# The order of the first loads: w1's first row split over two queues behind the x tiles, bias rows later

## The chip, the cores and the metric

The kernel runs on one core of one Trainium2 chip. The metric is the device time of one execution in microseconds; lower is better. A core has TensorE (PE in the profile, its weight loads apart as PEld), VectorE (DVE), ScalarE (ACT), GpSimd (POOL), and SyncE (SP), which here only issues DMAs. ScalarE can issue DMAs too, on a queue of its own, in order with its other instructions. All DMAs run on the same 16 DMA engines.

## The reference

```python
x = A_x                                           # 1 x 2048 x 512, bf16
g = sigmoid((x * gate_w).sum(-1, keepdims=True))
# a: linear attention, 32 heads of 16; phi(t) = where(t > 0, t + 1, exp(t)) + 1e-6
q, k, v = split(x @ wqkv)
o = (phi(q) @ (phi(k)^T v)) / (phi(q) . sum(phi(k)) + 1e-6)
a = o @ wo
# b: MLP over the tokens, F = 1792
h = layernorm(x)                                  # over the 512 features
u = gelu(einsum("bsd,sf->bdf", h, w1) + b1)
b = (einsum("bdf,fs->bds", u, w2) + b2) transposed back
return g * a + (1 - g) * b
```

## The kernel before

The 2048 tokens are 16 tiles of 128 (`NT`), the 512 features 4 blocks (`ND`), and the 1792 columns of w1 14 blocks of 128 (`NF`). The program has these stages, and TensorE goes through them in this order:

- 18 warm-up matmuls on a constant tile (L185), which need no data.
- MLP 1, first part (L277 to L283): u's first 8 blocks (`NFA`), accumulated in 8 PSUM banks over the 16 token tiles. Step t of the loop takes one token tile: 8 matmuls, one for each block of 128 columns of w1's row block t, all with the normalised tile `xh[:, t, :]`. The first 12 tiles go tile by tile; for the last 4 the order is block by block, so that each bank can be finished and its GELU started.
- k and the Gram product (L320 to L329), from x turned by DMA transposes and from `pk`.
- the other 6 blocks of MLP 1, mixed with q (L476 to L498), then y = u times w2 with the attention's product added into the same banks (L548 to L564).

Here "w1's row t" is the 128 x 1024 part that step t takes (`w1A[:, t, :]`, 256 KB in bf16), and its "blocks" 0 to 7 are the 128 columns each that the 8 matmuls take as weights. Every matmul goes through one helper, so all of TensorE's work is line L74; every DMA goes through `load`, line L124.

LayerNorm runs on VectorE and ScalarE, one tile after the other: `ln_bn` (BATCH_NORM_STATS, L195) reads the x tile, `ln_aggr` (L198) makes mean and variance, ScalarE takes the square root (L200), then `ln_apply` makes the reciprocal (L206) and `xh` (L208). The work on VectorE is in an order written by hand (`pin` keeps the program's order): the first half of tile t + 1's statistics stands in front of tile t's reciprocal and apply for t = 0 and t = 2.

The loads at the start, all of the functions named above being called in this order:

- ScalarE's queue: b1's rows (3.5 KB) into `b_rows`, then block 0 of w1's row 0 (32 KB), then an activation on one column (L136) whose only use is that the square root's table is loaded early.
- SyncE's queue: x tile 0, x tile 1 (128 KB each), blocks 1 to 7 of w1's row 0 (224 KB), w1's row 1, x tile 2, x tile 3, w1's row 2, and from there x tile t + 1 and w1's row t in turn. b2's rows stand behind w1's row 4. Behind them come the gate's weights, wk, 16 transposes of x, w1's other columns, wv, wo and wq.

The loads of the first loop wait for no data. The DMAs share eight semaphores, which are given out in turn, so that each waits until the one eight before it has landed.

`b_rows` holds b1 and b2 as rows; at tile 8 of LayerNorm, VectorE turns them into columns (L234 to L236), which GELU and the last scaling use.

w2's second half (columns 1024 to 2047) comes in pieces of its 14 row blocks while VectorE normalises q tile by tile (L508 to L514). It takes the place of w1's other columns, so its first piece waits for their last reader. Between the pieces stand the stores of q (`q_dram`) and, every four tiles, the transposes that bring q back (`turn`). The first y tile that reads the second half is tile 8.

Of the kernel before, what the change touches and what calls it, by code (L numbers as in the profile page):

```python
# [15 lines left out]
def kernel(  # L16
# [13 lines left out]
    nc = tc.nc  # L30
    P = nc.NUM_PARTITIONS
# [11 lines left out]
    NF = F // P  # L43
# [4 lines left out]
    FA = NFA * P  # L48
# [5 lines left out]
    w1_view = B_w1.rearrange("(t p) f -> p t f", p=P)  # L54
    w2_view = B_w2.rearrange("(f p) s -> p f s", p=P)
    b1_view = B_b1.rearrange("(f p) -> f p", p=P)
# [9 lines left out]
    def ptile(shape, dt, name):  # L66
        return persist.tile(shape, dt, name=name, tag=name)
# [27 lines left out]
    b_rows = ptile([32, P], BF16, "b_rows")  # L95
# [22 lines left out]
    w1A = wpool.tile([P, NT, FA], BF16, name="w1A", tag="w1st")  # L118
# [4 lines left out]
    def load(o, i, eng=None, **kw):  # L123
        pin((eng or nc.sync).dma_start(out=o, in_=i, **kw))  # L124

    def load_x(t0, t1):
        load(xr[:, t0:t1, :], x_view[:, t0:t1, :])

    def load_w1a(t):
        load(w1A[:, t, :], w1_view[:, t, 0:FA])  # L130


    tbl = work.tile([P, 1], FP32, name="tbl", tag="tbl", bufs=2)
    load(b_rows[0:NF, :], b1_view, nc.scalar)
    load(w1A[:, 0, 0:P], w1_view[:, 0, 0:P], nc.scalar)
    pin(nc.scalar.activation(out=tbl[:], in_=eps_t[:], func=ACT.Sqrt))  # L136

    load_x(0, 1)
    load_x(1, 2)
    load(w1A[:, 0, P:FA], w1_view[:, 0, P:FA])  # L140
    load_w1a(1)
    load_x(2, 3)
    for t in range(2, NT):
        if t + 1 < NT:
            load_x(t + 1, t + 2)
        load_w1a(t)
        if t == 4:
            load(b_rows[NF : NF + NT, :], b2_view)
    load(gw_b[:], gw_row_view.to_broadcast([P, D]))
    load(wk_sb[:], wqkv_view[:, :, D : 2 * D])  # L150
# [354 lines left out]

    pieces = {0: ((0, 4), (4, 7)), 5: ((7, 9),), 7: ((9, NF),)}  # L508
    for t in range(12):
        normalise(t)  # L510
        if t % 4 == 3:
# [83 lines left out]
```

## Time and profile before

| | |
|---|---|
| time before, median of 3 runs | 163.27 us (162.86 to 163.67) |
| the profiled execution | 163.07 us |
| its span, first to last instruction | 161.4 us |
| clock granted to TensorE | full |
| TensorE busy | 157.6 us (98%) |
| VectorE, ScalarE busy | 118.7 us (74%), 53.1 us (33%) |
| first matmul of MLP 1 | at 4.99 us |
| last matmul | ends at 158.5 us |
| DMA moved | 28.33 MB, mean 176 GB/s |

The profile is one execution; its times are microseconds from the first instruction. A group's line gives the engine, the operation, what is written and read, how often, and the idle time before it with what ended it. `SPq` and `ACTq` are the issues of DMAs on the two queues: the time in such a row is the issue alone, and the tile's own view gives the time from issue to landing. The share of busy time on TensorE is that of a pipelined engine whose ends are modelled: a matmul of 512 columns shows as 0.38 us, but the next one starts 0.216 us after it.

### The profile page before, as it was taken

How to read it: one execution, taken by the hardware profiler on the slowest of the kernel's cores; microseconds unless marked ns; L12 is line 12 of the kernel's file. 1: busy time of each engine (PE TensorE's matmuls, PEld its weight loads, DVE VectorE, ACT ScalarE, POOL GpSimd, SP SyncE). 2: the span in 40 equal slices, each digit the busy share in tenths (PEclk: the TensorE clock that was granted, in tenths of full speed). 3: DMA queues.
4: the chain of work that ended last, by engine and by line, in shares of the span. 5: the costliest groups of instructions: out<-in, count | busy, mean ns of one | idle time of the engine just before them, and what ended most of it. 6: DMA issues, size and time to landing. Idle time of an engine off the chain costs nothing.

```text
span 161.4 us, 2274 instructions
## 1 busy us (share of the span) xinstructions
PE 157.6 (98%) x820; PEld 73.1 (45%) x820; DVE 118.7 (74%) x278; ACT 53.1 (33%) x89; POOL 1.2 (1%) x8
## 2 busy tenths in 40 slices
PE   7999999999999999999999999999999999999993
PEld 5444444444444444444444444444444444444452
DVE  2799998959999998899895999999999970000002
ACT  4122227794342321434225970000008300550050
POOL 2000000000000000000000000000000000000000
PEclk9999999999999999999999999999999999999999
DMA  4999999444699630229952007826525935744421
GB/s 124 308 342 351 341 283 149 108 103 106 158 391 391 149 123 0 87 50 300 399 214 67 0 33 262 290 66 154 174 65 124 340 89 126 230 143 100 151 98 33
DMA packets 36838, 28.33 MB, mean 176 GB/s; under 512 B 20444, under 2 KB 31196, under 8 KB 36828
## 3 DMA queue, kind: packets, MB, share of 16 engines
q1 hardware_dynamic: 36384, 27.90, 57.6%
q10 hardware_dynamic: 444, 0.30, 0.6%
q8 instruction: 6, 0.10, 0.3%
q14 instruction: 4, 0.03, 0.0%
HBM read 19.28 MB, written 4.46 MB: 147 GB/s over the span
## 4 chain that ended last, share of the span: by engine, by line
PE 95%; DMA 2%; ACTq 0%; DVE 0%; issue 0%; DVEq 0%
PE yps L74 39%; PE accA L74 17%; PE accB L74 13%; PE qacc L74 9%; PE Gps L74 9%; PE kacc L74 9%; DMA w1A<-in_B_w_dram 2%; ACTq L124 0%; PE kvps L74 0%; DVE ot L539 0%; PE w2ps L74 0%; DVE b_rows L114 0%; DVEq L539 0%; DVE eps_t L115 0%
## 5 line engine op out<-in xcount | busy, mean ns | idle before, releaser
L74 PE MATMUL yps<-uT,w2h 128*128 128x512 bf16 (+2 forms) x238 | 49.2, 366 | 0.0
L74 PEld LDWEIGHTS <-w2h 128*128 128x128 bf16 x238 | 22.8, 98 | 25.9
L74 PE MATMUL accA<-xh,w1A 128*128 128x512 bf16 x128 | 28.0, 381 | 0.1
L532 ACT ACTIVATE ot<-yps,c,c 128x512 bf16<-128x512 f32 x15 | 11.6, 777 | 46.9 <-PE yps L74 34.8
L74 PE MATMUL accB<-xh,w1B 128*128 128x512 bf16 x96 | 21.5, 379 | 0.0
L539 DVE TENSOR_SCALAR ot<-yps,c,c 128x384 bf16<-128x384 f32 (+1 forms) x2 | 1.1, 542 | 25.5 <-PE yps L74 25.5
L74 PEld LDWEIGHTS <-w1A 128*128 128x128 bf16 x128 | 12.6, 98 | 15.6 <-DMA w1A<-in_B_w_dram 0.6
L74 PEld LDWEIGHTS <-xT 128*128 128x128 bf16 x128 | 12.3, 98 | 14.9 <-issue 0.2
L74 PE MATMUL Gps<-pk,xr 128*128 128x512 bf16 x64 | 15.8, 379 | 0.0
L74 PE MATMUL kacc<-wk_sb,xT 128*128 128x512 bf16 x64 | 15.8, 379 | 0.0
L74 PE MATMUL yps<-W2sb,pqT 128*128 128x512 bf16 (+2 forms) x68 | 14.6, 366 | 0.0
L74 PEld LDWEIGHTS <-w1B 128*128 128x128 bf16 x96 | 9.4, 98 | 11.3
L74 PE MATMUL qacc<-wq_sb,xT 128*128 128x512 bf16 x64 | 14.5, 379 | 0.0
L288 ACT ACTIVATE e<-qacc 128x512 bf16<-128x512 f32 x16 | 9.6, 597 | 12.2 <-DVE kvbdT L436 4.6
L288 ACT ACTIVATE e<-kacc 128x512 bf16<-128x512 f32 x16 | 9.2, 598 | 12.7 <-DVE pk L295 6.8
L290 DVE TENSOR_SCALAR e<-e 128x512 bf16<-128x512 bf16 x32 | 9.2, 288 | 4.6 <-ACT e L288 4.3
L195 DVE BATCH_NORM_STATS2 stats<-xr 128x6 f32<-128x512 bf16 (+1 forms) x18 | 10.9, 608 | 2.1 <-DMA xr<-in_A_x_dram 2.1
L408 DVE SCALAR_TENSOR_TENSOR pq<-pq,odds,rd 128x512 bf16<-128x512 bf16 x16 | 12.0, 752 | 0.6
L404 DVE TENSOR_REDUCE den<-prod 128x32 f32<-128x544 f32 x16 | 11.5, 720 | 0.6
L295 DVE SCALAR_TENSOR_TENSOR pk<-kacc,e 128x512 bf16<-128x512 f32 x16 | 11.1, 692 | 1.0
L295 DVE SCALAR_TENSOR_TENSOR pq<-qacc,e 128x512 bf16<-128x512 f32 x16 | 11.1, 692 | 0.6
L247 DVE CUSTOM_DVE_ANT_0 junk<-xr,gw_b 128x512 bf16<-128x512 bf16 x16 | 11.0, 690 | 0.5
(52 smaller groups left out, 95.5 us busy)
## 6 DMA issues: line engine op xcount, KB each, us to landing
w1A<-in_B_w_dram SPq DMA_DIRECT2D x15, 256.0 KB, 4.1
w2h<-in_B_w_dram SPq DMA_DIRECT2D x2, 1792.0 KB, 9.6
w1B<-in_B_w_dram SPq DMA_DIRECT2D x4, 768.0 KB, 7.6
xr<-in_A_x_dram SPq DMA_DIRECT2D x16, 128.0 KB, 4.0
q_dram<-pq SPq DMA_DIRECT2D x16, 128.0 KB, 3.4
out_dram<-ot SPq DMA_DIRECT2D x15, 128.0 KB, 1.9
w2h<-in_B_w_dram SPq DMA_DIRECT2D x1, 1280.0 KB, 6.7
w2h<-in_B_w_dram SPq DMA_DIRECT2D x1, 1024.0 KB, 5.1
```

What stands on the lines that cost most here:

```text
L74: nc.tensor.matmul(o, lhsT=lhsT, rhs=rhs, start=start, stop=stop, **kw)
L195: pin(nc.vector.bn_stats(out=stats[t][:, h, :], in_=xr[:, t, d0:d1]))
L247: nc.vector.tensor_tensor_reduce(out=junk[:], in0=xr[:, t, :], in1=gw_b[:], scale=1.0, scalar=0.0, op0=ALU.mult, op1=ALU.add, accum_out=gp ...
L288: pin(nc.scalar.activation(out=e[:], in_=acc[:], func=ACT.Exp))
L290: nc.vector.tensor_scalar(out=e[:], in0=e[:], scalar1=1.0, scalar2=PHI_EPS, op0=ALU.min, op1=ALU.add)
L295: nc.vector.scalar_tensor_tensor(out=o, in0=acc[:], scalar=0.0, in1=e[:], op0=ALU.max, op1=ALU.add)
L404: pin(nc.vector.tensor_reduce(out=den[:], in_=prod[:], op=ALU.add, axis=AX.X))
L408: nc.vector.scalar_tensor_tensor(out=heads, in0=heads, scalar=odds[:, t : t + 1], in1=rd[:].unsqueeze(2).to_broadcast([P, NH, HEAD]), op0= ...
L532: nc.scalar.activation(out=ot[:, d0:d1], in_=yps[:, d0:d1], func=ACT.Identity, scale=c1[:, t : t + 1], bias=c2[:, t : t + 1],)
L539: nc.vector.tensor_scalar(out=ot[:, d0:d1], in0=yps[:, d0:d1], scalar1=c1[:, t : t + 1], scalar2=c2[:, t : t + 1], op0=ALU.mult, op1=ALU.add,)
```

## The change

- b1's rows leave ScalarE's queue and stand on SyncE's, behind w1's row 4 and ahead of b2's rows.
- Row 0 of w1 comes in three loads in place of two: block 0 (32 KB) on SyncE behind x tile 0, blocks 1 to 3 (96 KB) on SyncE behind x tile 1, blocks 4 to 7 (128 KB) on ScalarE behind the table load and the one-column activation.
- The first two pieces of w2's second half (row blocks 0 to 3 and 4 to 6) are one load.

SyncE's queue has one more DMA ahead of x tile 1, of w1's row 1 and of all that follows, two more from x tile 6 on, and one less of them from w2's second half on. Nothing changes in the order of the work on TensorE and VectorE.

```diff
@@ -131,13 +131,13 @@
     tbl = work.tile([P, 1], FP32, name="tbl", tag="tbl", bufs=2)
-    load(b_rows[0:NF, :], b1_view, nc.scalar)
-    load(w1A[:, 0, 0:P], w1_view[:, 0, 0:P], nc.scalar)
     pin(nc.scalar.activation(out=tbl[:], in_=eps_t[:], func=ACT.Sqrt))
+    load(w1A[:, 0, FA // 2 : FA], w1_view[:, 0, FA // 2 : FA], nc.scalar)
 
     load_x(0, 1)
+    load(w1A[:, 0, 0:P], w1_view[:, 0, 0:P])
     load_x(1, 2)
-    load(w1A[:, 0, P:FA], w1_view[:, 0, P:FA])
+    load(w1A[:, 0, P : FA // 2], w1_view[:, 0, P : FA // 2])
     load_w1a(1)
     load_x(2, 3)
     for t in range(2, NT):
@@ -145,6 +145,7 @@
             load_x(t + 1, t + 2)
         load_w1a(t)
         if t == 4:
+            load(b_rows[0:NF, :], b1_view)
             load(b_rows[NF : NF + NT, :], b2_view)
@@ -505,7 +506,7 @@
-    pieces = {0: ((0, 4), (4, 7)), 5: ((7, 9),), 7: ((9, NF),)}
+    pieces = {0: ((0, 7),), 5: ((7, 9),), 7: ((9, NF),)}
```

## The prediction

> **What bounds the kernel now.** I read the page's chain of waits first, then the same chain in order of time:
>
> ```profile
> 0.99 0.03 DVE eps_t L115
> 1.02 0.63 ACTq L124
> 1.65 0.04 issue
> 1.69 3.26 DMA w1A<-in_B_w_dram
> 4.94 0.05 issue
> 4.99 28.02 PE accA L74 x128
> 33.01 4.32 PE kacc L74 x20
> ...
> 96.33 62.22 PE yps L74 x306
> 158.55 0.04 DVEq L539
> ```
>
> From 4.99 to 158.55 us the chain is TensorE alone. Only what lies ahead of 4.99, and gaps hidden inside the first group, can be won; the end after 158.55 is untouched. Next the timeline from 0.5 to 6.7 us (start, duration, engine, what):
>
> ```profile
> 0.80 0.87 SPq L124 DMA_DIRECT2D xr<-in_A_x_dram  x2
> 1.02 0.63 ACTq L124 DMA_DIRECT2D b_rows<-in_B_b_dram  x1
> 1.69 0.39 ACTq L124 DMA_DIRECT2D w1A<-in_B_w_dram  x1
> 1.72 0.91 SPq L124 DMA_DIRECT2D w1A<-in_B_w_dram  x2
> 2.10 1.28 ACT L136 ACT_TABLE_LOAD   x1 [2.10 <-issue]
> 2.67 0.91 SPq L124 DMA_DIRECT2D xr<-in_A_x_dram  x2
> 3.40 0.20 ACT L136 ACTIVATE tbl<-eps_t 128x1 f32<-128x1 f32 x1
> 3.75 0.39 DVE L195 BATCH_NORM_STATS2 stats<-xr 128x6 f32<-128x256 bf16 x1
> 4.39 0.41 DVE L208 TENSOR_SCALAR xh<-xr,mv,rstd 128x512 bf16<-128x512 bf16 x1
> 4.99 1.63 PEld L74 LDWEIGHTS <-w1A 128*128 128x128 bf16 x8 [0.63 <-DMA w1A<-in_B_w_dram]
> 6.55 0.69 DVE L195 BATCH_NORM_STATS2 stats<-xr 128x6 f32<-128x512 bf16 x1 [0.19 <-DMA xr<-in_A_x_dram]
> ```
>
> The first matmul had its xh tile at 4.39 + 0.41 = 4.80 and waited for w1's block 0 until 4.94. That load was ScalarE's second; its issue began at 1.69, behind the 0.63 us of the bias row. Block 1's load, issued on sync at 1.72, took 3.4 us to land by the w1A tile's view: about 5.15. Two fine windows of TensorE's timeline show what that did:
>
> ```profile
> 4.99 0.61 PE L74 MATMUL accA<-xh,w1A 128*128 128x512 bf16 x1
> 5.39 0.64 PE L74 MATMUL accA<-xh,w1A 128*128 128x512 bf16 x2
> ```
>
> The second matmul starts 0.40 us after the first, the third at 5.65. The steady step is 0.216 (four kacc matmuls take 0.86 in the chain), so 0.40 + 0.26 - 2 x 0.216 = 0.23 us is lost to blocks 1 to 7. Together with 4.99 - 4.84 = 0.15 (4.80 plus some 0.04 us of handover, as between the aggregate's end at 3.83 and the square root at 3.87), at most 0.38 us can be won: 0.23%.
>
> **What is late next.** Step t of the first loop needs xh tile t. The third tile, and the DVE rows after it:
>
> ```profile
> 8.02 0.41 DVE L208 TENSOR_SCALAR xh<-xr,mv,rstd 128x512 bf16<-128x512 bf16 x1
> ...
> 9.67 0.41 DVE L208 TENSOR_SCALAR xh<-xr,mv,rstd 128x512 bf16<-128x512 bf16 x1
> ```
>
> Step 1 starts at 5.65 + 6 x 0.216 = 6.94 and has xh tile 1 from 6.36: 0.58 to spare. Step 2 starts at 8.67, xh tile 2 is there at 8.43: 0.24. Step 3 starts at 10.40, xh tile 3 is there at 10.08: 0.32. After that VectorE makes a tile in 1.18 us and TensorE uses one in 1.73, so the margin grows. If step 2's tile stays where it is, the win is cut to 0.24 - 0.04 = 0.20 us. That tile hangs on x tile 2's landing (6.55, where VectorE waited 0.19), and the change moves that load.
>
> **The change, part by part.**
>
> *Block 0 on sync behind x tile 0.* Issue at about 1.26 instead of 1.69. With x tile 0's 2.1 us it lands at 3.4, with the 3.3 us of the ScalarE load at 4.6. Both are before 4.80, so block 0 no longer ends the wait: -0.15 us.
>
> *x tile 1 one slot later.* An issue takes 0.40 to 0.45 us, so x tile 1 goes from 1.26 to 1.72 and lands at 3.8 (2.1 us) instead of 3.35. VectorE starts on it at 3.75, in front of the reciprocal and apply of tile 0. Cost 0.05 us at 2.1 us. Were it as slow as the 3.4 of the load issued at 1.72 before, it would land at 5.1 and push everything by 1.4; but that load is 224 KB and shared the engines with block 0's; the row nearest is x tile 1's own. I take 0.05 to 0.1, upper end 0.35. First matmul at about 4.9.
>
> *Blocks 1 to 3 on sync behind x tile 1.* Issue 2.18 instead of 1.72, but 96 KB instead of 224. With the 3.4 us of the larger load it lands at 5.6, with 2.1 at 4.3. They are wanted at 5.1. I take 5.0: the 0.23 us gap mostly goes. If it stays, step 2 comes at the first matmul plus 3.68, 8.58, still 0.09 better than now.
>
> *Blocks 4 to 7 on ScalarE behind the table load.* The table load has no wait and can begin at about 0.85: 0.85 + 1.28 + 0.01 + 0.20 = 2.34 for the issue. Wanted at 4.9 + 4 x 0.216 = 5.77. With 3.3 to 3.5 us to landing, as the w1 loads issued from 1.69 to 2.20 show, it lands at 5.65 to 5.85. As step 2 can't start before 8.47, block 4 may start as late as 8.47 - 12 x 0.216 = 5.88 for nothing, and until 6.08 it costs no more than what is won. Cost taken: 0; it is the tightest term.
> The Trainium skill (ScalarE: Activation LUTs, What ACT_TABLE_LOAD costs) counts 1.28 us of load plus 1.38 us of drain for each switch of tables. By it the issue would be at 3.7 and the landing at 7.1; here the next activation starts 0.02 us after the load's end, and no drain is to be seen.
>
> *x tile 2 and the rest of sync's queue.* One issue more stands ahead of w1's row 1 and x tile 2: 2.20 to 2.65 and 2.67 to 3.12. The bytes ahead of x tile 2 are the same 768 KB, and in half-microsecond stretches from 3.5 us on the DMA engines show 0.75 to 1.16 busy, so its landing is set by bytes more than by its issue; it took 3.9 us. Bounds: -0.2 (less mixed small packets) and +0.45 (a full slot). I take +0.05. Step 2 then starts at 8.43 + 0.05 + 0.04 = 8.52: -0.15 us against 8.67.
> The Trainium skill (DMA: Bandwidth & Descriptors, Issuing engines are not separate DMA queues) says that a second queue saves issue time alone, as all share the engines; that is how x tile 2 is counted here.
>
> *Bias rows late.* ScalarE loses an issue of 0.63 us; sync gains one of about 0.36 before x tile 6. The rows are read at 14.80 (the four transposes); landing at 6.5 + 3.8 = 10.3 leaves 4 us. In the built program each DMA from the ninth waits for the landing of the one eight before it, and w1's row 4 now waits for ScalarE's load; x tile 6 and later may land 0.4 to 0.8 later. By then TensorE has over 1.5 us of margin to xh. Nothing; without that cover, up to 0.8.
>
> *One load of w2's second half in place of two.* Sync saves an issue of about 0.45 us at 96.4; the same 1792 KB go ahead of the same stores. The first reader is y tile 8 at 127.25, the landing about 105: 20 us of cover. Nothing.
>
> **Sum.** -0.15 us (-0.38 to +0.45 from the terms above). The profiled run took 163.07 (span 161.4 and 1.67 around it), so 162.92; the median of the three runs is 0.20 above it: 163.27 - 0.15 = 163.1.
>
> **The rivals.**
> 1. *The whole gap goes* (0.10): x tile 2 lands 0.15 or more earlier because block 0's small packets are out of the way, and step 2 starts at 8.30: -0.38, 162.9. For it: VectorE's wait of 0.19 at 6.55 is that load's. Against: the later issue.
> 2. *The slot is paid in full* (0.20): x tile 2 lands 0.45 later. xh tile 2 at 8.88, step 2 at 8.92: +0.25, 163.5. For it: sync issues without a pause up to 5.95. Against: its loads took 3.9 us, not 2.1, so they queued. Deciding point: from a landing 0.20 later on the kernel is slower.
> 3. *Blocks 4 to 7 come late* (0.12): ScalarE's load takes the 4.9 us of later w1 loads (issued at 9 to 11 us) and lands at 7.25; block 4 at 7.3, step 2 at 9.9: +1.2, 164.5; at 4.0 us it lands at 6.34, +0.3. It decides from a landing at 6.0 on. For it: the tight sum above. Against: ScalarE's queue has nothing ahead of it. (By the Trainium skill's switch of 2.66 us, named above, it would be +1.1.)
> 4. *The change is not seen* (0.08): x tile 1 lands at 4.1 and the start stays at 5.0 or 5.2: within 0.1 of now, 163.3.
>
> **Numbers.** The forecast, -0.25 to 0.0, has 0.50. 0.5% is 0.82 us, about what a measurement of this kernel can tell from no change; the three runs differ by 0.81. No case wins 0.82, as 0.38 is all that is idle; 0.06 is left for scatter. Slower by 0.82 takes the worse half of rival 3, scatter, and the worst of rivals 2 and 3 together: 0.13. The rest, 0.81, is within 0.5%. The range takes the terms' bounds (-0.38, +0.45) and 0.2 to 0.3 us of scatter of a median: 162.6 to 164.0.
>
> **What would show it.** Right: the first matmul at 4.85 to 4.95, the second 0.22 later, step 2 waiting for xh at about 8.5, and the first kacc matmul at 32.7 instead of 32.84. Wrong: a LDWEIGHTS of w1A waiting for a DMA at the fifth matmul (rival 3), the BN_STATS of x tile 2 after 6.75 (rival 2), or any TensorE gap after 33 us, where none is forecast.

## The result and the profile after

| | before | after |
|---|---|---|
| median of 14 runs each, us | 163.16 (162.67 to 163.67) | 164.22 (163.28 to 165.68) |
| profiled execution: time, span, us | 163.07, 161.4 | 164.54, 162.8 |
| x tile 1, issue and landing, us | 1.26, 3.33 | 1.72, 4.99 |
| first matmul of the first loop, us | 4.99 | 6.00 |
| first kacc matmul, us | 32.84 | 33.62 |
| wait for w2 at y tile 8, us | none | 0.69 |

The ratio of the times is 1.0081 [1.0057, 1.0106]: the change makes the kernel 1.06 us slower by the medians, where 0.15 us were forecast as a gain. The times of before form one group. Those of after form two: seven from 163.28 to 163.91, then the profiled one alone at 164.54, and six from 165.10 to 165.68. The ratios here and below are estimated over the runs without any that is more than 1.5% above the fastest of its kernel (165.96 of after_again, 166.13 of after_wide), and are not the quotients of the medians.

The timeline of the changed kernel from 0.5 to 10.5 us (start, duration, engine and line, what; in brackets the idle time before and what ended it):

```profile
0.80 1.28 ACT L134 ACT_TABLE_LOAD   x1 [0.80 <-PEq L580]
1.05 0.39 ACTq L124 DMA_DIRECT2D w1A<-in_B_w_dram  x1
1.26 0.41 SPq L124 DMA_DIRECT2D w1A<-in_B_w_dram  x1
1.72 0.43 SPq L124 DMA_DIRECT2D xr<-in_A_x_dram  x1
2.09 0.20 ACT L134 ACTIVATE tbl<-eps_t 128x1 f32<-128x1 f32 x1
5.01 0.43 DVE L196 BATCH_NORM_STATS2 stats<-xr 128x6 f32<-128x256 bf16 x1 [0.96 <-DMA xr<-in_A_x_dram]
5.53 0.41 DVE L209 TENSOR_SCALAR xh<-xr,mv,rstd 128x512 bf16<-128x512 bf16 x1
6.00 4.69 PE L74 MATMUL accA<-xh,w1A 128*128 128x512 bf16 x21 [1.66 <-DVE xh L209]
```

ScalarE's load of blocks 4 to 7 stands behind the table load and the activation in the program, and went out at 1.05, while the table load was still running. So the words "in order with its other instructions", further up, can't be read as waiting until those ahead are done; whether ScalarE had already taken the activation in by then, the trace doesn't say. This DMA was the second under way, ahead of block 0 (1.26) and of x tile 1 (1.72). x tile 1 then took 3.3 us to land where it had taken 2.1. VectorE's statistics row waited for it until 5.01, and that row stands ahead of the reciprocal and the apply of tile 0 on VectorE: a load of tile 1 held up tile 0. TensorE idled for 1.66 us. The chain in order of time names the same load where before it named w1's block 0:

```profile
1.72 3.26 DMA xr<-in_A_x_dram
```

TensorE's waits (us in total, times, longest) show both losses; the second is the last piece of w2's second half (row blocks 9 to 13):

```profile
PE accA L74 <- DVE xh L209: 1.7, 1, 1.7
PE yps L74 <- DMA w2h<-in_B_w_dram: 0.5, 1, 0.5
```

On TensorE's timeline around y tile 8 it looks so:

```profile
129.11 1.03 PE L74 MATMUL yps<-uT,w2h 128*128 128x512 bf16 x4
130.66 0.82 PE L74 MATMUL yps<-uT,w2h 128*128 128x512 bf16 x3 [0.52 <-DMA w2h<-in_B_w_dram]
```

Four matmuls at 0.216 from 129.11 make the next one due at 129.97; it started at 130.66, 0.69 late. The sum over the profiled execution: 1.01 for the later start, less 0.23 that before lost in its first matmuls and after did not, is 0.78, the shift of the first kacc matmul; with 0.69 it is 1.47, which is 164.54 - 163.07.

### The profile page after: what moved, and what is told of

Read it like the earlier page. It is cut to its first block, busy times and chain, and to the rows that moved or that the text cites. A ratio compares the mean times of both kernels' runs of the same rounds, so it can differ in the third digit from the quotient of the medians.

```text
span 162.8 us, 2261 instructions
## 1 busy us (share of the span) xinstructions
PE 156.3 (96%) x806; PEld 72.8 (45%) x820; DVE 118.6 (73%) x278; ACT 52.9 (33%) x89; POOL 1.2 (1%) x8
## 4 chain that ended last, share of the span: by engine, by line
PE 63%; DVE 20%; DMA 10%; SPq 4%; issue 1%; ACT 1%; DVEq 0%
PE yps L74 18%; PE accA L74 13%; PE kacc L74 9%; PE accB L74 8%; PE Gps L74 8%; PE qacc L74 6%; DMA w2h<-in_B_w_dram 5%; DVE pq L409 4%; DVE den L405 4%; SPq L124 4%; DVE prod L400 3%; DMA q_dram<-pq 3%; DVE pq L296 2%; DVE stats L196 2%; DMA xr<-in_A_x_dram 2%; DVE rd L407 2%
```

## The experiments

All ratios are against the kernel before on the same chip, whose medians were 163.04 to 163.10. The theories, by their letters in the expectations: x tile 1 is late because ScalarE's load goes out early and is ahead of it (A); or because the small loads of block 0 and blocks 1 to 3, with rows of 256 and 768 bytes, hold up SyncE's queue (B); w2's merge causes the wait at y tile 8 (C), or chance does (D); the turn of TensorE's clock decides between the groups (E); x tile 2 is the next load to be late (G).

**act_held: ScalarE's load made to wait for the activation.** The activation writes one column of the tile that the load fills, so the load has to come behind it.

```diff
-    pin(nc.scalar.activation(out=tbl[:], in_=eps_t[:], func=ACT.Sqrt))
+    pin(nc.scalar.activation(out=w1A[:, 0, FA // 2 : FA // 2 + 1], in_=eps_t[:], func=ACT.Sqrt))
     load(w1A[:, 0, FA // 2 : FA], w1_view[:, 0, FA // 2 : FA], nc.scalar)
```

> The changed kernel, with ScalarE's load of blocks 4 to 7 really held back: the one-column activation writes its result into the place that this load fills, so the load must wait for it. Theory A (ScalarE's load did not wait for the table load; issued at 1.05 us it put 128 KB ahead of x tile 1, which landed at 4.99): here it is issued at about 2.3, x tile 1 lands at 3.8 to 4.1, the first MLP matmul starts at 4.9 to 5.0 and the first kacc matmul at 32.6 to 32.9 (33.63 in the changed kernel), a time of 163.1 to 163.5 unless the later wait for w2 stays. Theory B (block 0's load of 256-byte rows, standing ahead of x tile 1 on sync, made it late): x tile 1 still lands at 4.7 to 5.0, first matmul at 5.7 to 6.0, no gain on 164.2.

Measured: 163.64 (163.13 to 165.43), ratio 1.0051 [1.0028, 1.0074]. Its timeline:

```profile
1.73 0.42 SPq L124 DMA_DIRECT2D xr<-in_A_x_dram  x1
2.32 0.39 ACTq L124 DMA_DIRECT2D w1A<-in_B_w_dram  x1
3.90 0.43 DVE L196 BATCH_NORM_STATS2 stats<-xr 128x6 f32<-128x256 bf16 x1
4.89 4.99 PE L74 MATMUL accA<-xh,w1A 128*128 128x512 bf16 x19
7.14 0.69 DVE L196 BATCH_NORM_STATS2 stats<-xr 128x6 f32<-128x512 bf16 x1 [0.75 <-DMA xr<-in_A_x_dram]
```

x tile 1, issued at the same moment as in the changed kernel, lands at 3.88, and the first matmul starts at 4.89, the forecast's 4.9. Then the next load is late: x tile 2 lands at 7.11 (6.53 before), step 2 starts at 9.08 (8.67 before). Of these 0.41 us only 0.15 are TensorE waiting for xh, since the last matmul of step 1 started at 8.71 and the next was due at 8.93. By the other 0.26 it was behind already, through matmuls 0.43 us apart up to 6.1 (more on these below). The first kacc matmul comes at 33.25, so the kernel is still slower than before. One run, 165.43, lies with the upper group of after; no trace of it is kept.

**x1_first: x tile 1 put ahead of block 0.**

```diff
     load_x(0, 1)
-    load(w1A[:, 0, 0:P], w1_view[:, 0, 0:P])
     load_x(1, 2)
+    load(w1A[:, 0, 0:P], w1_view[:, 0, 0:P])
```

> The changed kernel, with x tile 1 ahead of block 0 on sync again; ScalarE's load stays where it is. Theory A: x tile 1 is issued at 1.26, just behind ScalarE's 128 KB, and lands about 0.4 us (128 KB at 300 GB/s) later than the 3.33 of the kernel before, 3.7 to 4.2: first matmul 4.85 to 5.1, most of the front's 0.8 us is won back. Theory B: x tile 1 lands at 3.3 to 3.5 as before and block 0 is the late one (4.5 to 5.0): first matmul at 4.85 to 5.05. The landing of x tile 1 tells them apart, not the time: both 163.1 to 163.5 unless the later wait for w2 stays.

Measured: 163.23 (163.12 to 164.13), ratio 1.0021 [1.0008, 1.0034]. ScalarE's load goes out at 1.04 as in the changed kernel, but x tile 1 is issued at 1.26 and lands at 3.68:

```profile
1.04 0.39 ACTq L124 DMA_DIRECT2D w1A<-in_B_w_dram  x1
3.72 0.41 DVE L196 BATCH_NORM_STATS2 stats<-xr 128x6 f32<-128x256 bf16 x1
4.83 5.10 PE L74 MATMUL accA<-xh,w1A 128*128 128x512 bf16 x21
```

The pause is gone by this too. So neither an early load on ScalarE nor a slot more for x tile 1 brings the late landing by itself; the two together do. Its fastest runs take 163.12 where the kernel before has 162.68 to show; what holds them there is open.

**front_only and merge_only: the two ends of the change apart.** front_only is the changed kernel with w2's pieces as before; merge_only is the kernel before with nothing changed but the merge.

```diff
-    pieces = {0: ((0, 7),), 5: ((7, 9),), 7: ((9, NF),)}
+    pieces = {0: ((0, 4), (4, 7)), 5: ((7, 9),), 7: ((9, NF),)}
```

> The changed kernel with w2's second half in its old pieces (0 to 4 and 4 to 7 apart). Theory C (the one big load causes the wait of 0.68 us for w2's last piece at y tile 8): that wait is gone, the front's 0.8 us stays: 163.9 to 164.1 in every run, no runs above 165. Theory D (the last piece has next to no margin, 128.95 against 129.2 us in the profile before, and lands later by chance or with the late front): wait and time as in the changed kernel, 163.3 to 165.7 with the two groups of runs.

> The kernel before with only the two loads of w2's second half made one. Theory C: front as before (first MLP matmul at 4.99 us), but a wait for w2's last piece at y tile 8, and 163.6 to 165 with a spread of over 1.5 us. Theory D: as before, 162.7 to 163.7, no wait over 0.3 us at y tile 8.

Measured: front_only 163.64 (163.43 to 165.79, two of twelve above 165.7), ratio 1.0062 [1.0032, 1.0092]; x tile 1 lands at 4.92, the first matmul starts at 5.93, the first kacc at 33.56, and nothing waits for w2, whose last piece lands at 129.22. merge_only 163.30 (162.94 to 164.05), ratio 1.0016 [0.9999, 1.0033], with no wait for w2 either. Most of the loss belongs to the front: 1.0062 of 1.0081. What is left is of the size of merge_only's 1.0016, but the intervals are too wide to tell it from nothing. merge_only showed what was missing in the account: its whole front is that of before and its second load of w1 lands at 4.43, ahead of the first matmul (4.82), yet its matmuls step by 0.43 us until 6.9. The windows view, stretch by stretch (us, length, then busy share and number of instructions of PE, PEld, DVE, ACT and POOL, the granted clock, the DMA share and GB/s; the number counts all that touch the stretch):

```profile
5.00:6.00 1.00, 1.00 (x3) 0.29 (x2) 0.57 (x4) 0.30 (x1) 0.00 (x0) 1.00 0.99 251
6.00:7.00 1.00, 1.00 (x4) 0.39 (x3) 0.72 (x2) 0.00 (x0) 0.00 (x0) 1.00 0.85 255
7.00:8.00 1.00, 1.00 (x7) 0.43 (x5) 0.92 (x4) 0.29 (x1) 0.00 (x0) 1.00 0.98 326
```

TensorE is busy all the time and does half as much up to 6.9. The granted clock reads 1.00 in all three rows, so it doesn't show this; the number of matmuls does.

**after_again: the changed kernel once more,** to see an execution of the upper group.

> The changed kernel once more, for a second profile and more times. Theory E (TensorE's clock starts at half rate and turns to full at a moment that differs from run to run, seen at 3.5 to 6.9 us in six profiles by the step from 0.213 us for 256 columns to 0.11, or from 0.43 for 512 to 0.216; a pause of 1.65 us before the first MLP matmul can put the turn off by another stretch of some 3.4 us): two groups of runs again, near 163.6 and near 165.4, and a profile of the upper group would show the first 8 to 16 MLP matmuls 0.43 us apart, a lower one 0.216 from the first. Theory D for the w2 wait (chance): a wait at y tile 8 in some runs only; if this profile has none, the 0.68 us seen before is not the change's.

Measured: 164.52 (163.33 to 165.96), ratio 1.0079 [1.0044, 1.0113]; again six runs from 163.33 to 163.89 and six from 165.16 to 165.96. The profiled one took 165.41. Its windows, and those of the first profile of the changed kernel behind them:

```profile
5.00:6.00 1.00, 0.39 (x2) 0.11 (x2) 0.93 (x5) 0.00 (x0) 0.00 (x0) 1.00 1.08 262
7.00:8.00 1.00, 1.00 (x4) 0.30 (x2) 0.97 (x4) 0.04 (x1) 0.00 (x0) 1.00 0.97 307
8.00:9.00 1.00, 1.00 (x4) 0.33 (x3) 0.92 (x4) 0.26 (x1) 0.00 (x0) 1.00 1.06 390
10.00:11.00 1.00, 1.00 (x7) 0.41 (x5) 0.96 (x5) 0.29 (x1) 0.00 (x0) 1.00 1.06 348
```

```profile
5.00:6.00 1.00, 0.00 (x0) 0.00 (x0) 0.96 (x4) 0.00 (x0) 0.00 (x0) 1.00 0.88 258
7.00:8.00 1.00, 1.00 (x7) 0.45 (x5) 0.96 (x3) 0.00 (x0) 0.00 (x0) 1.00 0.89 302
```

Here the first matmul came earlier than in the other profile (5.61 against 6.00), the pause was shorter (0.77 against 1.66), and nothing waited for w2; still this execution is 0.87 us longer. Its matmuls step by 0.43 until 9.5: (9.5 - 5.61) / 2 = 1.95 us lost. 1.95 - 0.39 - 0.69 = 0.87, the whole difference. In the other profile the clock had turned at about 3.6, within the warm-up (18 warm-up matmuls took 3.50 us there, 4.00 here), and the pause did no more harm than its own length.

**after_w24 and before_w10: the pause closed, and a pause made.** after_w24 is the changed kernel with 24 warm-up matmuls for 18, so that TensorE stays busy up to the first loop; before_w10 is the kernel before with range(10) in the same line.

```diff
-    for _ in range(18):
+    for _ in range(24):
```

> The changed kernel with 24 warm-up matmuls for 18, so that TensorE at half rate is busy until 5.95 us and has no pause before the first MLP matmul at 6.0. Theory E: the upper group of runs (165.1 to 165.8) is gone, all between 163.3 and 164.3, median 163.7. Rival F (the upper group comes from later, from w2's last piece or another wait): both groups stay, as nothing after 6 us changes.

> The kernel before with 10 warm-up matmuls for 18: TensorE idles from about 3.0 to 4.85 us, the loads stay as they are. Theory E: an upper group of runs appears, some 1.7 us (half of 3.4) above the others, so times from 162.7 to 165.5 with a gap, in about half of the runs. Rival F: no upper group; 162.7 to 163.7 as the kernel before, at most 0.4 more for a clock that turns later.

Measured: after_w24 163.60 (163.21 to 164.13), ratio 1.0034 [1.0016, 1.0052]; none of its twelve runs is in the upper group, though its first matmul is as late as 5.91 and its clock turned at about 6.5. before_w10 165.37 (164.93 to 166.28), ratio 1.0151 [1.0120, 1.0183]; all of its six runs lie up there, where half of them were expected. Its loads are those of before and its first matmul starts at 4.82, behind a pause of 1.69 us, as long as the 1.66 of the first profile of the changed kernel, where the clock had already turned; and:

```profile
7.00:8.00 1.00, 1.00 (x4) 0.35 (x3) 0.93 (x3) 0.29 (x1) 0.00 (x0) 1.00 0.95 349
8.00:9.00 1.00, 1.00 (x5) 0.39 (x4) 0.92 (x4) 0.00 (x0) 0.00 (x0) 1.00 1.02 363
9.00:10.00 1.00, 1.00 (x6) 0.45 (x5) 0.96 (x4) 0.29 (x1) 0.00 (x0) 1.00 0.99 363
```

Half rate until 8.3, without any change of a load. So a pause in TensorE's work ahead of the first loop can put off the turn of the clock. Without a pause, or with the turn ahead of it, the turn was seen between 3.6 and 6.9. Three profiles have a pause that began before the turn: behind 0.77 us (after_again) it came at 9.5, behind 1.69 us (before_w10) at 8.3, but behind 0.52 us (after_wide, below) at 5.7. A pause as short as that did not put it off; how long one has to be was not tried. before_w10 also waited for w2's last piece (0.4 us in TensorE's waits), with w2's pieces as before: that wait doesn't need the merge.

The Trainium skill (TensorE: Matmul & The Clock Gate, Part 1: The HAM clock gate) says that a cold TensorE runs at half rate until a window of 3413 ns was busy, and that these windows run freely, so that the turn comes at another moment in each run. The runs agree: the turns without a pause lie 6.9 - 3.6 = 3.3 us apart, no more than one such window. With windows at any phase, a pause from 4.84 on would catch at most those that end between 4.84 and 6.9, (6.9 - 4.84) / 3.4 = 0.6 of the runs by estimate, and fewer as far as a short pause catches none. In the upper group were 12 of the 26 runs of the changed kernel, and 2 of 12 of front_only, which has the same front. The pause of before_w10 began at 3.13, ahead of every end seen: all six.

**bias_late: only b1's rows moved to SyncE.**

```diff
-    load(b_rows[0:NF, :], b1_view, nc.scalar)
     load(w1A[:, 0, 0:P], w1_view[:, 0, 0:P], nc.scalar)
...
         if t == 4:
+            load(b_rows[0:NF, :], b1_view)
             load(b_rows[NF : NF + NT, :], b2_view)
```

> The kernel before with one part of the change alone: b1's rows behind w1's row 4 on sync, so that block 0's load is the first on ScalarE's queue, issued at about 0.85 instead of 1.69. x tile 1 keeps its slot. If block 0 was what the first matmul waited for: it lands before 4.2, first matmul at 4.82 to 4.85 in every run; the half-rate clock covers much of the rest, so 162.8 to 163.3, 0 to 0.15 us better than before. If its small packets delay x tile 1 (issued at 1.26), x tile 1 lands at 3.6 to 4.0 and the first matmul at 4.85 to 5.1: no gain or a loss of 0.1 to 0.2.

Measured: 163.34 (162.86 to 163.81), ratio 1.0016 [1.0000, 1.0032]; profiled 162.91. Block 0 is issued at 0.80 and lands at 3.16, x tile 1 at 3.48, and the first matmul starts at 4.94, now behind xh. Freeing block 0 in this way wins nothing that can be measured.

**act_held_x2: act_held with x tile 2 ahead of w1's row 1.**

```diff
-    load_w1a(1)
     load_x(2, 3)
+    load_w1a(1)
```

> The changed kernel with ScalarE's load held back (as act_held, 163.64 us) and x tile 2 ahead of w1's row 1 on sync. Theory G (what is left of the loss in act_held is x tile 2, which landed at 7.11 for 6.53 before, so that step 2 started at 9.08 for 8.67): x tile 2 lands by 6.3, step 2 follows step 1 with no wait, the first kacc matmul at 32.6 to 33.0 by the moment of the clock's turn, time 163.0 to 163.3. Rival H (x tile 2 is late because of the DMAs' rate at 5.5 to 6.5 us, not of its place): it still lands after 6.8, no gain on 163.6. A gain on 163.07 is not expected.

Measured: 163.56 (163.13 to 164.17), ratio 1.0023 [1.0007, 1.0040]. Step 2 no longer waits for x tile 2, but x tile 1 lands at 4.11 and the first matmul starts at 5.12, and w1's row 1 lands at 7.01 and holds up step 1 by 0.21. The first kacc matmul comes at 32.97. In this stretch a load that is brought forward makes another one late.

**after_wide: blocks 0 and 1 in SyncE's first load (rows of 512 bytes), 2 and 3 in the second.**

```diff
-    load(w1A[:, 0, 0:P], w1_view[:, 0, 0:P])
+    load(w1A[:, 0, 0 : 2 * P], w1_view[:, 0, 0 : 2 * P])
     load_x(1, 2)
-    load(w1A[:, 0, P : FA // 2], w1_view[:, 0, P : FA // 2])
+    load(w1A[:, 0, 2 * P : FA // 2], w1_view[:, 0, 2 * P : FA // 2])
```

> The changed kernel with the first two loads of w1's row 0 on sync cut at block 2 in place of block 1: rows of 512 bytes and 64 KB, then again 512 bytes and 64 KB. Theory A (128 KB of ScalarE's load ahead of x tile 1 made it late): x tile 1 has 32 KB more ahead and lands at 4.4 to 5.1 as in the changed kernel, both groups of runs stay. Theory B (256-byte rows slow the queue): x tile 1 lands at 3.8 to 4.2, first matmul by 5.2, hardly a run above 164.5.

Measured: 163.41 (163.22 to 166.13, one run in the upper group), ratio 1.0021 [1.0005, 1.0036]; x tile 1 lands at 4.34, the first matmul starts at 5.36. The four profiles with the front as changed have landings of 4.99, 4.59, 4.92 and 4.33, so 4.34 lies inside their spread. Whether short rows are a part of the delay is left open. TensorE's rows up to 8 us, and those of after_again behind them, show what a shorter pause did; in both all 18 warm-up matmuls had run at half rate:

```profile
5.36 2.89 PE L74 MATMUL accA<-xh,w1A 128*128 128x512 bf16 x12 [0.52 <-DVE xh L209]
5.61 2.72 PE L74 MATMUL accA<-xh,w1A 128*128 128x512 bf16 x6 [0.77 <-DVE xh L209]
```

Behind 0.52 us of pause twelve matmuls fit where six did behind 0.77: the clock turned at about 5.7.

**merge_again: merge_only once more.**

> The kernel before with only the two loads of w2's second half made one, a second time: the first gave a ratio of 1.0016 (0.9999 to 1.0033). Theory D (the merge does nothing): a ratio of 0.999 to 1.001. Theory C (the merge costs some 0.2 us in the mean by a wait for w2 in some runs): again 1.001 to 1.003.

Measured: 163.17 (162.80 to 164.47), ratio 1.0022 [1.0000, 1.0044], again with no wait for w2. Both intervals of the merge touch 1: it costs between nothing and some 0.5 us, and no place in the two profiles shows it. Two of these runs, 164.40 and 164.47, lie above every run of before (at most 163.82), so a cost in some runs is not ruled out.

**x2_early: the kernel before with x tile 2 ahead of w1's row 1,** a try at a better version (the diff is that of act_held_x2).

> The kernel before with x tile 2 ahead of w1's row 1 on sync, all else as before; a try at a version better than both. x tile 2 lands at 5.8 to 6.2 instead of 6.5, w1's row 1 at 6.0 to 6.3, wanted at 6.6. Where the clock turns before the first MLP matmul, step 2 then no longer waits for xh at 8.47 and 0.1 to 0.2 us are won; where it turns later, nothing. 162.9 to 163.1 in the median, 0 to 0.2 better than the kernel before; if w1's row 1 becomes the late one, 0.1 to 0.3 worse.

Measured: 163.04 (162.76 to 163.45), ratio 0.9999 [0.9987, 1.0012]. x tile 2 lands at 4.63 instead of 6.53 and nothing is won. No version was found that beats the kernel before.

## Why the prediction was wrong

- **Blocks 4 to 7 on ScalarE: the step that failed.** The forecast issued this load at 2.34, behind the table load and the activation; it went out at 1.05 with the table load running from 0.80 to 2.08. Nothing ties the load's data to either, and its issue waited for neither. Where the data did tie them (act_held) it was issued at 2.32. The trace of before could not warn of it, since there both ScalarE loads stood ahead of the table load; the forecast took the order of the program for the order of time. The term was called tightest on the side of lateness, and it failed by coming early.
- **x tile 1 one slot later.** Taken at 0.05 to 0.1 with 0.35 as the upper end; it cost 1.01 at the first matmul. The text had the far end in hand (3.4 us, landing at 5.1, "push everything by 1.4") and set it aside for tile 1's own row of 2.1 us. That row holds where ScalarE's load is held back (2.1 us to landing in act_held); with it and block 0 ahead, 3.3 us was right.
- **The 0.23 us gap "lost to blocks 1 to 7".** Misread. It was TensorE at half rate: merge_only shows the same 0.43 steps with all of the load landed. In bias_late, where the clock had turned in the warm-up and blocks 1 to 7 landed at 5.19, the second matmul came 0.296 after the first, so there the load cost 0.08. The gap did go in the profile of after, because the clock had turned early in that execution, not because of the new order.
- **What the forecast did not have at all: the clock's turn.** It is large enough for the spread of before (a turn at 6.9 costs (6.9 - 4.99) / 2 = 0.96 us, and the times reach from 162.67 to 163.67), and with a pause ahead of the first loop it makes the upper group of after, about 1.8 us above the lower one. Of the 1.06 us between the medians, the lower group has some 0.4 (163.5 against 163.1): with the late x tile 1 alone the forecast would have had the sign wrong, and the rest came through the half of the runs in the upper group. That the clock decides is shown by after_w24 and before_w10; in which window of a given run the turn falls is not in the trace.
- **The merge of w2, forecast at nothing.** "20 us of cover" was the first piece's. The last piece, which the merge leaves as it was, landed at 128.95 before and was due at 129.20 (129.97 - 0.78): 0.25 of cover. In the profile of after its issue came 0.89 later (123.15) and it took 7.5 us instead of 6.7. front_only, as late at its front, had it at 129.22 and did not wait, so the 0.69 is this execution's and not in every run; whether the merge makes it likelier is open. A TensorE gap after 33 us was named as what would show the forecast wrong, and it was there.
- **What held.** Block 0 on SyncE no longer ends the wait (landed at 3.62). The first matmul at 4.9 is right for the issue time that was assumed (4.89 in act_held). Bias rows late made nothing wait. The table load shows no drain behind it: the next activation comes at 2.09, against a load that ends at 2.08, and in the trace of before each of the three later table loads (24.52, 33.75, 91.09) is followed by an activation 0.01 us after its end. The issue at 3.7 that was reckoned from the Trainium skill's 2.66 us for a switch (ScalarE: Activation LUTs, What ACT_TABLE_LOAD costs) was not borne out. The 2.34 reckoned without the drain was met only where the data tied the load to the activation (2.32 in act_held).
- **The rivals.** Rival 2's mechanism, x tile 2 late, was there in the profile of after (6.76, 0.23 later than before, past its deciding point of 0.20), but TensorE was later still: step 2 came at 9.45 and had its tile from 9.29. It made TensorE wait only once ScalarE's load was held: 7.11, 0.58 later than before, and 0.15 at step 2. Rival 3 had the right load, and the reverse of its mechanism. The 1.4 us case stood in the text without a chance of its own; it should have been the rival on the other side.

## What to carry to other kernels

A DMA's place in an engine's program is no time: ask what data ties its issue to the instructions ahead of it, and where nothing does, take it as issued at once, as here at 1.05, and count what it then overtakes. A load that the first instructions of a serial chain need goes ahead of bulk loads on every queue, since here 0.46 us more at the issue, behind 128 KB from the other queue, became 1.66 us at the landing; without those 128 KB ahead it was 0.55 (act_held). And the warm-up of TensorE should reach up to the first real matmul: behind pauses of 0.77 and 1.69 us that began at half rate, 1.9 and 1.8 us went into slow matmuls that no wait shows (29.56 and 29.39 from the first matmul to the first kacc, against 27.62 in the profile of after).

## What the hardware showed that was not expected

- ScalarE issued a DMA at 1.05 to 1.44, in the middle of its own table load (0.80 to 2.08).
- TensorE at half rate is seen in the step between matmuls (0.43 for 0.216 us at 512 columns) and in their number for each microsecond (x4 for x7), while the granted clock reads 1.00. It turned at a moment between 3.6 and 6.9 us without a pause in the half-rate stretch, at 5.7 behind a pause of 0.52 us, and at 8.3 and 9.5 behind 1.69 and 0.77.
- In stretches of one microsecond of the fourteen profiles the DMA engines moved 150 to 366 GB/s from 3 to 6 us at a busy share of 0.65 to 1.08, and 279 to 392 from 8 to 10 us at 0.95 to 1.07. Why the first ones are slower was not tried.
